# A planner without the rule that keeps VectorE's conversions and GpSimdE's operations apart

## The chip, the cores and the metric

The kernel runs on one core of one Trainium2 chip, in one launch. TensorE (PE) multiplies, VectorE (DVE), ScalarE (ACT) and GpSimdE (POOL) do the elementwise work, and SyncE (SP) issues the DMAs; each engine takes its instructions in the order in which they are written, and waits where an operand or a buffer is not ready. The metric is the device time of one execution in microseconds; less is better.

## The reference

Three parts in a row: a linear attention with the delta rule over 768 steps (4 batches, 8 heads, 48 elements), an expert layer with a rational function, and one with a squared relu. Each expert layer has 3072 tokens, 384 inputs and 2048 inner elements. Cut to what is computed:

```python
k_n = k / (np.linalg.norm(k, axis=-1, keepdims=True) + 1e-06)
for t in range(S):
    kt, vt, bt = (k_n[:, :, t], v[:, :, t], beta[:, :, t, None])
    y[:, :, t] = np.einsum('bhd,bhde->bhe', q[:, :, t], state)
    v_old = np.einsum('bhde,bhd->bhe', state, kt)
    state = state + bt[:, :, :, None] * np.einsum('bhd,bhe->bhde', kt, vt - v_old)
...
h = x @ w_in
P = a[0] + a[1] * h + a[2] * h2 + a[3] * h3
Q = 1.0 + np.abs(b[0]) * np.abs(h) + np.abs(b[1]) * h2
x = (P / (Q + 1e-06)) @ w_out
...
r = np.maximum(x @ w_in, 0.0)
return (r * r) @ w_out
```

Inputs and outputs are the host's arrays as they are; the expert weights arrive in 64-bit floating point and are turned into 32 bits on the chip with operations on integers.

## The kernel before

The 3072 tokens are cut into six stages of 512. For each stage i the attention of its steps is computed (group g = i, eight steps of 16 or 32 positions each), then layer 1 takes the stage's 512 columns through 16 pieces j of 128 inner elements. Layer 2 follows for all six stages.

The attention of a group has Gram products (L442, copied by ScalarE in L421), the norms (ScalarE L457, L458; VectorE L463 to L473, the head of the inverse), and the inverse of a triangular matrix. The inverse of g=0 and g=1 is a chain of 15 pairs of steps on VectorE (L479, L481), closed by two transposes (L514, L515); that of g=2 to 5 is a chain of 31 pairs on GpSimdE (L488, L492). Behind it TensorE takes the products L549, L560, L571, L597, L609 with copies by ScalarE (L429) or VectorE (L433) between, and VectorE's L553. Then come eight steps of the recurrence (TensorE L686, L745, L746; ScalarE L720, L739, L759; GpSimdE L724; VectorE L729, L764). GpSimdE scales the values in L641 and clears the tiles Tt and TT in L459 and L523.

One piece of layer 1 is: mm1 (L887, nine matmuls into one of three banks h), the rational function (ScalarE L904, L905, L906, then L910, L911 behind GpSimdE's L907; VectorE L908, L909, L912, L913 and L914, which writes the result), and mm2 (L923, three matmuls into the accumulators). Before a stage its columns are split into a high and a low part (ScalarE L870, VectorE L871). In layer 2 the function is L934 to L938 and the second product L947 to L949.

The weights of a piece come by DMA and are converted: ScalarE L829, VectorE L830, L831, L834 (the first matrix, A) and L836 (the second, B), then ScalarE L845 rounds A and GpSimdE L846 gives its low part.

No instruction is emitted directly. Every one is handed to a plan with its engine, an estimated duration, what it reads and writes, and a due time; conversions, steps of the inverse and several others carry `lock=1`. The plan's `play()` simulates the engines and always starts what can start earliest, with due times to choose; eight rounds are simulated, each with due times derived from the one before, and the order of the best is written out. Where the plan sees TensorE idle for long, filler matmuls (L283) are put there. No wait in the program enforces the plan's times; they only decide the order on each engine, which buffer an operation gets, and how many fillers there are.

## Time and profile before

| what | value |
|---|---|
| median of three runs | 1132.02 us (1125.41, 1132.02, 1133.59) |
| profiled execution | 1127.35 us |
| its span | 1125.6 us |
| TensorE busy | 1065.3 us, 95% |
| VectorE, ScalarE, GpSimdE busy | 673.7, 684.3, 387.8 us |
| mean granted TensorE clock | 0.966 |

All rows of the trace come from the one profiled execution. Times in it start with its span. A row of the timeline has the start, the length, the engine, the line, the operation, and the tiles with their shapes; "x3" joins three such instructions that follow each other, and the bracket at the end tells how long the engine was idle before and what it was released by. L907 in a row means line 907 of the kernel before.

### The profile page before, as it was taken

Reading aid. Unit: us, or ns where it says so; the run is one execution under the profiler, and the core shown is the slowest. Engines: PE = TensorE matmul, PEld = TensorE weight load, DVE = VectorE, ACT = ScalarE, POOL = GpSimd, SP = SyncE. Lnnn points to the kernel's source line nnn. Section 1 sums busy time; section 2 is a strip of 40 time slices with the busy share of each in tenths; the row PEclk is TensorE's granted clock in tenths of the full one; section 3 lists DMA queues with packets and bytes.
Section 4 is the critical chain, followed back from the end, with each engine's and each line's share of the span. In section 5 each row is a group of like instructions: output and inputs, shape, how many; then the busy total and the mean of one; then the engine's idle time right before and its main releaser. Section 6 shows DMA issues by size and latency. Waiting matters only on the chain.

```text
span 1125.6 us, 24712 instructions
## 1 busy us (share of the span) xinstructions
PE 1065.3 (95%) x10076; PEld 761.6 (68%) x10076; DVE 673.7 (60%) x1115; ACT 684.3 (61%) x1242; POOL 387.8 (34%) x540
## 2 busy tenths in 40 slices
PE   5688798789999999999999989999999999999998
PEld 5676565465666566666666556588888888888887
DVE  6567786777667756766666588887334343433332
ACT  4165687787788788777878697765334233332422
POOL 3314587628845862884233143425000000000000
PEclk7679899989999999999999999999999999999999
DMA  7464225560263055016000221441101010000000
GB/s 231 120 182 124 70 55 178 156 137 33 82 161 74 25 150 104 33 45 138 29 19 20 71 83 47 153 156 40 45 1 57 1 37 20 1 29 1 29 0 29
DMA packets 116065, 83.49 MB, mean 74 GB/s; under 512 B 83568, under 2 KB 101104, under 8 KB 115952
## 3 DMA queue, kind: packets, MB, share of 16 engines
q1 hardware_dynamic: 115952, 81.92, 25.5%
q8 instruction: 79, 1.29, 0.5%
q14 instruction: 34, 0.28, 0.1%
HBM read 62.88 MB, written 17.83 MB: 72 GB/s over the span
## 4 chain that ended last, share of the span: by engine, by line
PE 84%; ACT 4%; DVE 3%; issue 2%; POOL 0%; DMA 0%; SPq 0%; DVEq 0%; ACTq 0%; POOLq 0%
PE bank L887 34%; PE bank L923 21%; PE bank L949 6%; PE bank L947 6%; PE bank L948 6%; PE bank L686 5%; PE bank L745 2%; PE bank L597 1%; PE bank L609 1%; ACT mem L905 1%; ACT xin L759 1%; ACT mem L906 0%; DVE X L764 0%; ACT X L720 0%; DVE bank L913 0%
## 5 line engine op out<-in xcount | busy, mean ns | idle before, releaser
L887 PE MATMUL bank<-xh,A 128*128 128x512 f32 x1152 | 360.6, 394 | 1.1 <-POOL A L846 1.1
L923 PE MATMUL bank<-mem,B 128*128 128x512 f32 x576 | 278.6, 613 | 4.1 <-DVE mem L914 1.7
L887 PE MATMUL bank<-xl,A 128*128 128x512 f32 x576 | 257.6, 447 | 5.3 <-DVE mem L914 5.3
L887 PEld LDWEIGHTS bank<-xh,A 128*128 128x128 f32 x1152 | 218.4, 190 | 63.4 <-issue 16.0
L907 POOL TENSOR_TENSOR mem<-mem 128x512 f32<-128x512 f32 x96 | 123.3, 1286 | 203.6 <-ACT mem L905 203.0
L923 PEld LDWEIGHTS bank<-mem,B 128*128 128x128 f32 x576 | 103.8, 192 | 96.9 <-issue 78.7
L935 DVE SCALAR_TENSOR_TENSOR mem<-bank,mem 128x512 f32<-128x512 f32 x96 | 66.2, 690 | 157.0 <-ACT mem L934 157.0
L934 ACT ACTIVATE mem<-bank 128x512 f32<-128x512 f32 x96 | 57.3, 598 | 159.9 <-PE bank L887 158.0
L887 PEld LDWEIGHTS bank<-xl,A 128*128 128x128 f32 x576 | 109.1, 189 | 47.2 <-issue 15.3
L949 PE MATMUL bank<-gh,C 128*128 128x512 f32 x288 | 113.7, 395 | 0.0
L947 PE MATMUL bank<-gl,C 128*128 128x512 f32 x288 | 113.5, 394 | 0.0
L948 PE MATMUL bank<-gh,C 128*128 128x512 f32 x288 | 111.9, 389 | 0.0
L912 DVE SCALAR_TENSOR_TENSOR mem<-mem,par,bank 128x512 f32<-128x512 f32 x96 | 71.4, 743 | 67.0 <-ACT bank L911 66.8
L938 DVE TENSOR_TENSOR gl<-mem,gh 128x512 fp32r<-128x512 f32 x96 | 67.4, 702 | 61.3 <-ACT gh L937 61.2
L937 ACT CAST gh<-mem 128x512 fp32r<-128x512 f32 x96 | 59.6, 621 | 68.5 <-DVE mem L935 57.3
L908 DVE TENSOR_TENSOR mem<-bank,mem 128x512 f32<-128x512 f32 x96 | 65.8, 686 | 57.5 <-ACT mem L906 57.2
L904 ACT ACTIVATE mem<-bank 128x512 f32<-128x512 f32 x96 | 57.0, 595 | 47.5 <-PE bank L887 46.6
L905 ACT ACTIVATE mem<-mem,par 128x512 f32<-128x512 f32 x96 | 77.8, 812 | 2.0
L910 ACT ACTIVATE mem<-mem,par 128x512 f32<-128x512 f32 x96 | 69.3, 722 | 15.2 <-POOL mem L907 13.9
L906 ACT ACTIVATE mem<-bank,par 128x512 f32<-128x512 f32 x96 | 73.6, 769 | 0.7
L492 POOL TENSOR_TENSOR Tt<-Tt,tmp 128x31 f32<-128x31 f32 (+15 forms) x124 | 70.3, 567 | 8.5
L488 POOL TENSOR_TENSOR tmp<-Gb,Tt 128x31 f32<-128x31 f32 (+15 forms) x124 | 66.1, 533 | 20.1 <-DVE Tt L473 12.1
(125 smaller groups left out, 1564.7 us busy)
## 6 DMA issues: line engine op xcount, KB each, us to landing
raw<-in_w_dram SPq DMA_DIRECT2D x18, 768.0 KB, 4.6
B<-in_w_dram SPq DMA_DIRECT2D x10, 768.0 KB, 6.6
kTg<-in_kS_dram SPq DMA_DIRECT2D x40, 128.0 KB, 2.8
gs<-Gs SPq DMA_DIRECT2D x40, 128.0 KB, 2.8
kTc<-in_kT_dram SPq DMA_DIRECT2D x40, 128.0 KB, 2.4
X<-in_qT_dram SPq DMA_DIRECT2D x96, 48.0 KB, 2.6
kn<-in_kn_dram SPq DMA_DIRECT2D x12, 384.0 KB, 4.2
vn<-in_vn_dram SPq DMA_DIRECT2D x12, 384.0 KB, 3.5
```

Of the source, the lines that this page charges most:

```text
L492: P_.tensor_tensor(Tt[:, 0:a, s + 1:32], Tt[:, 0:a, s + 1:32], tv, op=ALU.subtract)
L887: M.matmul(h, a, b, start=(k == 0 and m == 0), stop=(k == NK - 1 and m == 2))
L905: add("ACT", 0.83, lambda: A_.activation(b(), a(), AF.Identity, bias=s(4), scale=s(5)), r=[ak, "par"], w=[bk], due=due + 3.3, alloc=(("b", ...
L906: add("ACT", 0.79, lambda: A_.activation(c(), h(), AF.Identity, bias=s(2), scale=s(3)), r=[hk, "par"], w=[ck], due=due + 4.5, alloc=(("c", ...
L907: add("POOL", 1.32, lambda: P_.tensor_tensor(b(), b(), a(), op=ALU.mult), r=[ak], w=[bk], due=due + 4.2, lock=1)
L910: add("ACT", 0.72, lambda: A_.activation(a(), b(), AF.Ln, bias=s(6)), r=[bk, "par6"], w=[ak], due=due + 6)
L912: add("DVE", 0.75, lambda: V.scalar_tensor_tensor(c(), c(), s(0), h(), op0=ALU.add, op1=ALU.mult), r=[hk, "par"], w=[ck], due=due + 8)
L923: M.matmul(acc[d], Bw[j][:, 128 * d:128 * d + 128], slot[gk], start=(j == 0), stop=(j == NJ - 1))
L938: add("DVE", 0.72, lambda: V.tensor_tensor(gl(), b(), gh(), op=ALU.subtract), r=[bk, gk, "late"], w=[lk], due=due + 5, lock=1, alloc=(("gl ...
L947: M.matmul(acc[d], wh, gl, start=(j == 0), stop=False)
L948: M.matmul(acc[d], wl, gh, start=False, stop=False)
L949: M.matmul(acc[d], wh, gh, start=False, stop=(j == NJ - 1))
```

## The change

The plan no longer keeps VectorE's operations marked `lock=1` and GpSimdE's from overlapping: the variable that held the end of the last such operation on either engine is gone. The planned durations of three conversions on VectorE are raised. The operations handed to the plan stay the same.

```diff
         kept, frees, owner, reuse = {}, {}, {}, {}
-        lockend = {"DVE": 0.0, "POOL": 0.0}
         for t in T:
...
                 s = max(s, a[len(t["alloc"]) - 1])
-            if t["lock"]:
-                s = max(s, lockend["POOL" if t["eng"] == "DVE" else "DVE"])
             return s
...
                 free_at[e] = end if e != "LAND" else 0.0
-            if t["lock"] and e in lockend:
-                lockend[e] = end
             t["s"], t["e"] = s, end
...
-            add("DVE", 0.56, lambda: V.tensor_scalar(lo(), lo(), 29, None, op0=ALU.logical_shift_right), w=[rk], due=d0, lock=1)
+            add("DVE", 0.62, lambda: V.tensor_scalar(lo(), lo(), 29, None, op0=ALU.logical_shift_right), w=[rk], due=d0, lock=1)
...
-            add("DVE", 0.6, lambda: V.scalar_tensor_tensor(lo()[:, si], hi()[:, si], 3, lo()[:, si], op0=ALU.logical_shift_left, op1=ALU.bitwise_or),
+            add("DVE", 0.7, lambda: V.scalar_tensor_tensor(lo()[:, si], hi()[:, si], 3, lo()[:, si], op0=ALU.logical_shift_left, op1=ALU.bitwise_or),
...
-            add("DVE", 0.6, lambda: V.scalar_tensor_tensor(Bw[j].bitcast(U32), hi()[:, so], 3, lo()[:, so], op0=ALU.logical_shift_left, op1=ALU.bitwise_or),
+            add("DVE", 0.7, lambda: V.scalar_tensor_tensor(Bw[j].bitcast(U32), hi()[:, so], 3, lo()[:, so], op0=ALU.logical_shift_left, op1=ALU.bitwise_or),
```

The orders of all four compute engines change in the first 240 us; the number of fillers falls from 124 to 89. The lines of the new kernel's body are lower by 5: its L899 is L904 of the kernel before, its L903 is L908.

VectorE at the beginning of the first stage of layer 1 (a bank is the h of one piece j; `mem` is the rational function's storage, `raw` and `B` the weights being converted), before:

```order
L908 TENSOR_TENSOR mem<-bank_74,mem 128x512
L909 SCALAR_TENSOR_TENSOR mem<-mem,par,bank_74 128x512
L908 TENSOR_TENSOR mem<-bank_72,mem 128x512
L909 SCALAR_TENSOR_TENSOR mem<-mem,par,bank_72 128x512
L908 TENSOR_TENSOR mem<-bank_73,mem 128x512
L912 SCALAR_TENSOR_TENSOR mem<-mem,par,bank_74 128x512
L463 RECIPROCAL nbr<-nby 128x32
L464 TENSOR_TENSOR nbr<-nbr,Gb 128x32
L465 TENSOR_TENSOR nbr<-nbr,nby 128x32
L466 TENSOR_SCALAR nrm<-nbr 128x32
L467 RECIPROCAL nbr<-nrm 128x32
L468 TENSOR_TENSOR nbr<-nbr 128x32
```

and in the changed kernel:

```order
L903 TENSOR_TENSOR mem<-bank_73,mem 128x512
L904 SCALAR_TENSOR_TENSOR mem<-mem,par,bank_73 128x512
L829 SCALAR_TENSOR_TENSOR raw_104<-raw_104 128x384
L907 SCALAR_TENSOR_TENSOR mem<-mem,par,bank_73 128x512
L908 SCALAR_TENSOR_TENSOR bank_73<-mem,bank_73 128x512
L825 TENSOR_SCALAR B<-B 128x768
L903 TENSOR_TENSOR mem<-bank_72,mem 128x512
L904 SCALAR_TENSOR_TENSOR mem<-mem,par,bank_72 128x512
L826 SCALAR_TENSOR_TENSOR B<-B 128x768
L831 SCALAR_TENSOR_TENSOR B<-mem 128x384
L909 SCALAR_TENSOR_TENSOR mem<-bank_73,mem 128x512
```

Before, L908 and L909 of two pieces, and L908 of a third, stand ahead of the first L912, and the head of the inverse of g=2 (L463 to L473) ahead of the first L913. Now the first piece goes through to its L914 (here L909), with conversions between, and the head of the inverse has moved behind the fifth piece's.

ScalarE at the same place (`Gs` is a Gram product's copy, TT_112 an operand of the attention of g=1), before:

```order
L905 ACTIVATE mem<-mem,par 128x512
L421 COPY Gs_139<-bank_75 128x256
L905 ACTIVATE mem<-mem,par 128x512 x2
L910 ACTIVATE mem<-mem,par 128x512 x2
L845 CAST A_83<-raw_103 128x384
L429 COPY TT_112<-bank_75 32x16x32
L910 ACTIVATE mem<-mem,par 128x512
L429 COPY TT_112<-bank_75 32x16x32 x3
L906 ACTIVATE mem<-bank_74,par 128x512
L906 ACTIVATE mem<-bank_72,par 128x512
L906 ACTIVATE mem<-bank_73,par 128x512
```

and in the changed kernel:

```order
L899 ACTIVATE mem<-bank_73 128x512
L900 ACTIVATE mem<-mem,par 128x512
L901 ACTIVATE mem<-bank_73,par 128x512
L899 ACTIVATE mem<-bank_72 128x512
L416 COPY Gs_138<-bank_75 128x256
L905 ACTIVATE mem<-mem,par 128x512
L906 ACTIVATE bank_73<-mem 128x512
L900 ACTIVATE mem<-mem,par 128x512
L416 COPY Gs_139<-bank_75 128x256
L901 ACTIVATE mem<-bank_72,par 128x512
```

Before, L905 and L910 of three pieces and the copies L429 stand ahead of the first L906; now the first piece has its five operations (here L899, L900, L901, L905, L906) almost in a row.

GpSimdE during the inverse of g=0 (X are the recurrence's operands, vn the values, A the first weights), before:

```order
L523 MEMSET TT_111 32x32x32 x2
L459 MEMSET Tt 128x1024
L641 TENSOR_TENSOR vn_130<-vn_130,nT_125 128x768
L724 AFFINE_SELECT X_107<-X_107 64x4x64 x2
L724 AFFINE_SELECT X_108<-X_108 64x4x64 x2
L724 AFFINE_SELECT X_109<-X_109 64x4x64 x2
L641 TENSOR_TENSOR vn_131<-vn_131,nT_125 128x768
L724 AFFINE_SELECT X_110<-X_110 64x4x64 x2
L846 TENSOR_TENSOR A_79<-mem,A_79 128x384
```

and in the changed kernel:

```order
L719 AFFINE_SELECT X_107<-X_107 64x4x64 x2
L518 MEMSET TT_111 32x32x32 x2
L719 AFFINE_SELECT X_108<-X_108 64x4x64 x2
L719 AFFINE_SELECT X_109<-X_109 64x4x64 x2
L719 AFFINE_SELECT X_110<-X_110 64x4x64 x2
L841 TENSOR_TENSOR A_79<-mem,A_79 128x384
L636 TENSOR_TENSOR vn_130<-vn_130,nT_125 128x768
L636 TENSOR_TENSOR vn_131<-vn_131,nT_125 128x768
L454 MEMSET Tt 128x1024
```

The memset of Tt (L459, here L454) stands behind the inverse on VectorE, whose result lies in Tt; before, the L641, L724 and L846 stood behind it, now (L636, L719, L841) ahead of it.

## Rows read from the trace of the kernel before

**Rows 1.** The page, part 1: busy time, share of the span and instructions of each engine.

```profile
PE 1065.3 (95%) x10076; PEld 761.6 (68%) x10076; DVE 673.7 (60%) x1115; ACT 684.3 (61%) x1242; POOL 387.8 (34%) x540
```

**Rows 2.** The table of windows, cut at the first mm1 of the stages of layer 1 (the second row is a part of the first). Columns: the window and its length; busy time and instructions of PE, PEld, DVE, ACT and POOL; granted TensorE clock; share of the DMA engines; GB/s.

```profile
96.00:240.50 144.50, 124.69 (x1828) 82.90 (x1827) 104.00 (x171) 102.57 (x191) 88.92 (x114) 0.92 0.43 121
131.00:240.50 109.50, 97.80 (x1162) 61.04 (x1162) 79.21 (x128) 80.83 (x152) 70.72 (x89) 0.94 0.48 137
341.40:441.80 100.40, 100.40 (x1137) 62.86 (x1137) 67.91 (x118) 82.06 (x153) 62.42 (x97) 1.00 0.37 88
643.70:735.00 91.30, 86.04 (x284) 53.88 (x283) 74.85 (x108) 72.18 (x115) 35.93 (x30) 0.98 0.33 114
```

**Rows 3.** TensorE from 96 to 131, grouped by line (busy time, mean ns of one, idle time before it and its releaser); then rows of its timeline (start, length, line; in brackets the idle time before the row).

```profile
L283 PE MATMUL bank<-ones 128*128 128x256 bf16 x61 | 7.5, 273 | 0.0
...
L571 PE MATMUL bank<-DN,mem 32*32 32x32 f32 x128 | 3.1, 214 | 2.1 <-ACT TT L429 2.1
...
L597 PE MATMUL bank<-TT,TN 32*32 32x32 f32 x64 | 1.2, 192 | 0.8 <-ACT TN L429 0.8
L609 PE MATMUL bank<-ws,TN 32*32 32x32 f32 x64 | 1.2, 192 | 0.4 <-ACT ws L429 0.4
...
95.95 0.50 PE L887 MATMUL bank<-xl,A 128*128 128x512 f32 x1
...
127.06 1.93 PE L560 MATMUL bank<-mem,DN 32*32 32x32 f32 x128 [4.43 <-DVE mem L553]
...
130.62 4.71 PE L923 MATMUL bank<-mem,B 128*128 128x512 f32 x6
```

**Rows 4.** ScalarE's timeline in the first stage.

```profile
103.67 1.09 ACT L904 ACTIVATE mem<-bank 128x512 f32<-128x512 f32 x2
...
107.70 1.52 ACT L905 ACTIVATE mem<-mem,par 128x512 f32<-128x512 f32 x2
109.12 1.57 ACT L910 ACTIVATE mem<-mem,par 128x512 f32<-128x512 f32 x2
...
114.25 2.12 ACT L906 ACTIVATE mem<-bank,par 128x512 f32<-128x512 f32 x3
...
116.77 0.58 ACT L911 ACTIVATE bank<-mem 128x512 f32<-128x512 f32 x1
```

**Rows 5.** VectorE's timeline in the first stage.

```profile
115.13 0.69 DVE L908 TENSOR_TENSOR mem<-bank,mem 128x512 f32<-128x512 f32 x1 [9.70 <-ACT mem L906]
...
119.16 0.34 DVE L463 RECIPROCAL nbr<-nby 128x32 f32<-128x32 f32 x1
...
122.37 0.69 DVE L913 SCALAR_TENSOR_TENSOR bank<-mem,bank 128x512 f32<-128x512 f32 x1
...
129.48 1.87 DVE L914 SCALAR_TENSOR_TENSOR mem<-bank,mem 128x512 f32<-128x512 f32 x3
```

**Rows 6.** GpSimdE in the first stage (96 to 240.5), grouped by line; then the two groups of the inverse in the second stage (240.5 to 341.4); then the first and the last of the 62 operations of the inverse of g=2 in its timeline.

```profile
L907 POOL TENSOR_TENSOR mem<-mem 128x512 f32<-128x512 f32 x16 | 20.5, 1288 | 19.4 <-ACT mem L905 19.2
L492 POOL TENSOR_TENSOR Tt<-Tt,tmp 128x31 f32<-128x31 f32 (+15 forms) x31 | 20.0, 647 | 2.1
L488 POOL TENSOR_TENSOR tmp<-Gb,Tt 128x31 f32<-128x31 f32 (+15 forms) x31 | 19.3, 624 | 5.4 <-DVE Tt L473 3.6
L846 POOL TENSOR_TENSOR A<-raw,A 128x384 fp32r<-128x384 f32 x10 | 10.4, 1036 | 15.9 <-ACT A L845 8.8 <-issue 7.0
L724 POOL TENSOR_SCALAR_AFFINE_SELECT X<-X 64x256 f32<-64x256 f32 x17 | 8.5, 500 | 4.4 <-ACT X L720 3.4 <-POOL X L724 0.5
...
L492 POOL TENSOR_TENSOR Tt<-Tt,tmp 128x31 f32<-128x31 f32 (+15 forms) x31 | 16.8, 541 | 2.2
L488 POOL TENSOR_TENSOR tmp<-Gb,Tt 128x31 f32<-128x31 f32 (+15 forms) x31 | 15.6, 503 | 3.4 <-DVE Tt L473 1.3
...
122.55 0.24 POOL L488 TENSOR_TENSOR tmp<-Gb,Tt 128x31 f32<-128x31 f32 x1 [3.64 <-DVE Tt L473]
...
212.24 0.99 POOL L492 TENSOR_TENSOR Tt<-Tt,tmp 128x31 f32<-128x31 f32 x1
```

**Rows 7.** The start: GpSimdE's timeline, then the ends of VectorE's inverse of g=0.

```profile
34.40 1.16 POOL L459 MEMSET Tt<- 128x1024 f32 x1 [14.96 <-DVE DN L515]
...
37.07 4.32 POOL L724 TENSOR_SCALAR_AFFINE_SELECT X<-X 64x256 f32<-64x256 f32 x6
...
20.36 1.23 DVE L472 TENSOR_TENSOR Gb<-Gb,nbr 128x1024 f32<-128x1024 f32 x1
...
32.36 1.93 DVE L515 STREAM_TRANSPOSE DN<-Tt 128x1024 f32<-128x1024 f32 x1
```

**Rows 8.** Operations of VectorE beside and not beside one of GpSimdE: L834 at 88.46 with GpSimdE's L641, and L834 at 99.61; L481 with 128x120 elements at 72.72 with GpSimdE's L724, and at 24.74.

```profile
88.46 1.35 DVE L834 SCALAR_TENSOR_TENSOR mem<-mem 128x384 uint32<-128x384 uint32 x1
...
99.61 0.55 DVE L834 SCALAR_TENSOR_TENSOR mem<-mem 128x384 uint32<-128x384 uint32 x1
...
87.92 1.47 POOL L641 TENSOR_TENSOR vn<-vn,nT 128x768 f32<-128x768 f32 x1 [3.77 <-issue]
...
72.72 0.45 DVE L481 TENSOR_TENSOR Tt<-Tt,tmp 128x120 f32<-128x120 f32 x1
...
72.63 0.41 POOL L724 TENSOR_SCALAR_AFFINE_SELECT X<-X 64x256 f32<-64x256 f32 x1 [27.75 <-PE bank L686]
...
24.74 0.28 DVE L481 TENSOR_TENSOR Tt<-Tt,tmp 128x120 f32<-128x120 f32 x1
```

## Prediction

> **What bounds the kernel now.** I read the page first: TensorE is busy for 1065.3 of 1125.6 us [rows 1]. Where is it not? The table of windows cut at the first mm1 of each stage of layer 1 (240.5, 341.4, ...) tells it [rows 2]: from 341.4 to 441.8 busy equals the window, and the last stage of layer 1 is busy for 86.04 of 91.3. Only the first stage is long: 144.5 us (96 to 240.5, 124.69 of them busy) against 100.4 for a later stage. Order can win time in the first 240 us, hardly after them.
>
> Next, what the first stage waits for. TensorE's list and timeline of 96 to 137 [rows 3]: the first mm1 starts at 95.95, and the first mm2 only at 130.62, behind the attention products L560 (127.06) that wait 4.43 us for VectorE. Between them stand 61 filler matmuls (7.5 us), which the plan puts where it sees a gap. ScalarE's rows [rows 4] tell why: L904 of three j's, then L905 of three, L910 of three, then copies for the attention (L429), and only at 114.25 the L906 without which VectorE cannot go on. VectorE [rows 5] sat idle for 9.70 us before L908 at 115.13, then took L463 to L473 (119.16 to 122.4, the head of the inverse of g=2) ahead of L913, and gave the first L914 at 129.48, 33 us after the mm1 it belongs to. So the stage is late by its order, not by a lack of engines.
>
> **The change, part by part.** No operation is added or removed except about 35 fillers (124 to 89); only the planned order differs, since nothing but order kept the two engines apart. I set the two orders side by side and priced three places.
>
> *First stage.* In the new order ScalarE takes j=0 through L904, L905, L906, L910, L911, with one L904 and one copy L421 between, VectorE follows with L908, L909, L912, L913, L914 and six other operations between, and the head L463 stands behind the fifth L914. By hand, the first mm1 at 97: its bank is complete at about 100; L904 0.6, L905 0.76 (1.52 for two), GpSimdE's L907 1.25 (3.74 for three), L910 0.78 (1.57 for two), L911 0.58 and the two inserted operations (1 us) bring ScalarE to 105.4; L912 and L913 at 0.7 each, six others of 0.55 to 1.0 (3.5 together) and L914 at 0.62 bring the first L914 to 111 [rows 4, 5]. That is 18 us earlier than 129.5 (rows give every term but the 100).
> What is left for TensorE then: its window from 131 to 240.5 holds 97.8 us of work and 11.7 of idle [rows 2]; the attention products L571, L597, L609 (3.1 + 1.2 + 1.2 = 5.5 us), which ran before 131, come after 111 too [rows 3]. TensorE alone would be through at 111 + 98 + 5.5 = 214.5, with the old idle at 226. But the inverse of g=2, 62 operations on GpSimdE, can no longer begin at 122.55 [rows 6]: its head is now behind five L914, some 29 VectorE rows of 0.2 to 1.0 us after the first L914, about 17 to 18 us with waits beside, plus the head's own 3.2 to 3.5 [rows 5]; so it starts at about 138, 15.5 later. By the order 7 L907, 5 L846 and 16 L724 lie inside it. From their rows: 19.3 + 20.0 for the inverse, 7 x 1.29, 5 x 1.04, 16 x 0.50, together 61.5, with up to 5 of gaps 66.5 [rows 6]. It ends at 199.5 to 204.5, against 213.2. Before, 27.3 us lay between that end and the next stage; if 17 of these are work that must follow, this road ends the stage at 216.5 to 221.5; with all 27.3 at 227 to 232. I take 228, nearest to the old idle (226) and inside the second figure: 131 us for the stage, a gain of 12.5 against the old 240.5. Bounds: 222 (gain 18) and, where the inverse is slowed by another 6 and the full tail follows, 238 (gain 2).
>
> *Start.* In the old plan GpSimdE was idle for 14.96 us, until 34.40, while VectorE ran the g=0 inverse, from L472 (20.36) to L515 (32.36, through at 34.3); then came the memset, two L641 six L724 (4.32 together) and L846 [rows 7]. In the new order L724 x8, an L846 and both L641 stand ahead of the memset, so they run beside that inverse, which is on the path to the first mm1. What does an overlap cost? The trace has one clean case [rows 8]: L834 took 1.35 at 88.46 while L641 ran from 87.92 to 89.39, and 0.55 alone at 99.61; an inverse step (L481) took 0.45 beside an L724 of 0.41, against 0.28 alone. The VectorE operation is held until the GpSimdE one ends. The price lies between 0 (all collide with nothing that waits) and the full length of what overlaps, 1.04 for L846 [rows 6], 2 x 1.47 for L641, six L724 at 0.41, together 6.4. I take 4 for the large three, 1 for the small ones: 5, near the full end because the inverse is one unbroken chain of some 35 VectorE rows. Behind it wait L514, L515 and with them TensorE's L549, L560.
> The Trainium skill (SBUF — State Buffer, section Who interferes with whom) says that VectorE and GpSimdE share a port pair that is held for a whole instruction, that a VectorE operation with two SBUF inputs contends with a GpSimdE operation that reads SBUF, and that one with at most one SBUF input, outside the two-port modes, does not. The L834 row agrees; by the rule alone the start would lose all 6.4 where the sum has 5.
> More filler matmuls stand ahead of the first mm1 and two products L549 are placed before it: 28 fillers at 7.5 / 61 are 3.4 us [rows 3], but they fill a wait, so I count 1 (bounds 0 and 3.4).
>
> *The rest.* The raised costs (0.56 to 0.62, 0.6 to 0.7) are only plan numbers. In stage 1 copies L457 and the Gb loads stand earlier; I allow 0 to 1 of gain. Stages 2 to 5 and layer 2 keep long identical stretches, and TensorE is full there, which hides any exchange of VectorE rows: 0. Should the cover fail, the last stage's 5.3 us of idle is what such a stage costs.
>
> *Sum.* -12.5 + 5 + 1 - 0 = -6.5 on the profiled execution: 1127.35 to about 1121. That execution lies 4.7 under the median of the three runs (1132.02; they run from 1125.41 to 1133.59). I go half the way up and say 1123. A difference of 1% (11.3 us) is about what this kernel's measurement tells from no change.
>
> **Rivals.**
> 1. *Only TensorE limits the first stage and the start hides the overlap.* For: GpSimdE's operations wait for inputs from VectorE and ScalarE, and many could fall beside VectorE rows that read only one tile. Against: the steps of the inverse, most rows there, read two. Stage gain 18, start +1: -17, or 1110.
> 2. *Nothing comes of it.* The early L914 is given back, since the inverse of g=2 starts 15.5 later and the mm1s end up waiting for A pieces (L846) behind it on GpSimdE. For: GpSimdE has 66 us in a row there. Against: before, that inverse took 90.7 us with the same operations and had slack. Stage gain 5 to 6, start +6: 1127 to 1132.
> 3. *Slower: the overlap costs in full, at every place.* One mechanism: a VectorE operation with two inputs in SBUF waits out the GpSimdE operation beside it, and the other way round. At the start 6.4; in the g=1 inverse, also VectorE's, two L846 and two L641 come beside it, 2 x 1.04 + 2 x 1.47 = 5; in the first stage the g=2 inverse, whose operations already lost 39.3 - 32.4 = 7 us against the next stage [rows 6], loses 7 more, and a stage limited by GpSimdE ends 7 later. -12.5 + 7 + 11.4 + 1 = +7: 1134 by the profile, 1138 by the median, up to 1146. It decides once the start loses more than the stage gains: more than about 12 us of overlap on the path, or half of that with a stage gain of only 5. By the page cited above this full price is the expected one; the trace bears it out in a handful of operations, so it has its chance below, no more.
>
> **How the numbers follow.** My forecast, a few us faster: 0.40 (its own range 1115 to 1129). Rival 1: 0.20. Rival 2: 0.20. Rival 3: 0.20. Faster by over 1% (below 1120.7) takes rival 1 and a quarter of my case: 0.30. Slower by over 1% (above 1143.3) is the upper end of rival 3: 0.10 with its half. The rest, 0.60, is within 1%. The range leaves out the tail of rival 1 and of rival 3: 1109 to 1140.
>
> **What would show it.** Right: in the changed kernel's trace the first mm2 follows the first mm1 by about 14 us instead of 34.7; the first stage is 127 to 136 us long instead of 144.5; the first mm1 comes at 99 to 103; fewer fillers after it; layer 2 about as long as before. In the g=0 inverse some VectorE rows are lengthened to the end of a GpSimdE row. Wrong: a first stage under 127 or over 140; a start later by more than 8 or not at all; a later stage that is 3 us or more longer than its 100, which I priced at nothing.

## The result, and the profile after

| | before | after |
|---|---|---|
| median | 1127.23 us (20 runs, 1120.12 to 1133.59) | 1135.36 us (20 runs, 1130.75 to 1141.96) |
| profiled execution | 1127.35 us | 1130.75 us |
| mean granted TensorE clock of it | 0.966 | 0.970 |

The ratio is 1.0074 with the interval [1.0057, 1.0091]: about 8 us slower, where 6.5 us faster was forecast between the profiled executions. The profiled execution of before lies at its median; that of after is the fastest of its 20. So two sums are kept apart below: the two traces differ by 3.4 us, the medians by 8.1.

The page of the changed kernel, part 1 [rows 1], and its windows [rows 2]: the first stage, a later stage, the last stage of layer 1, and 20 us around the first products of layer 2. Columns as in [rows 2].

```profile
PE 1068.4 (95%) x10041; PEld 760.0 (67%) x10041; DVE 689.3 (61%) x1115; ACT 683.4 (61%) x1242; POOL 397.2 (35%) x540
...
100.11:237.54 137.43, 122.36 (x1831) 78.57 (x1829) 100.63 (x160) 102.75 (x191) 85.55 (x112) 0.93 0.49 135
237.54:338.30 100.76, 99.42 (x1120) 62.09 (x1119) 73.40 (x122) 81.81 (x153) 64.17 (x96) 1.00 0.35 87
640.40:726.30 85.90, 78.83 (x247) 46.82 (x245) 73.18 (x102) 68.85 (x111) 38.77 (x30) 0.98 0.30 103
720.00:740.00 20.00, 16.02 (x60) 10.69 (x59) 19.43 (x21) 12.74 (x23) 13.95 (x10) 1.00 0.83 291
```

The same 20 us of the kernel before:

```profile
720.00:740.00 20.00, 20.00 (x78) 14.23 (x77) 16.95 (x24) 13.45 (x25) 7.15 (x7) 1.00 0.77 277
```

The first mm1 of the second and of the fifth stage before, and of the fifth stage after:

```profile
239.96 0.79 PE L887 MATMUL bank<-xl,A 128*128 128x512 f32 x1
...
541.32 0.79 PE L887 MATMUL bank<-xl,A 128*128 128x512 f32 x1
...
539.51 0.79 PE L882 MATMUL bank<-xl,A 128*128 128x512 f32 x1
```

The same operations take VectorE 15.6 us longer (689.3 against 673.7) and GpSimdE 9.4 longer: the overlap lengthens them. Cut at the first mm1 of each stage, the two traces differ at four places: the first mm1 comes 4.16 us later (100.11 against 95.95 [rows 3]); the first stage is 6.6 us shorter (137.43 against 144.01, 95.95 to 239.96); the next three stages give back 0.6, so that the fifth stage begins 1.8 earlier than before; and on the way into layer 2 TensorE loses 5.2, after which layer 2 stays 3.4 late to the end. In the two windows of 720 to 740 is the surprise: TensorE, full before, now has 3.98 us of idle in 20, and VectorE is busy for 19.43 of them. The orders differ there too: they change not only in the first 240 us, but at places in the later stages, and on all engines again between 650 and 795.

**The start.** Timelines of the changed kernel [rows 7]: GpSimdE's rows beside the inverse of g=0, VectorE's steps beside them and one of the same shape later, and TensorE's first product behind the inverse.

```profile
18.67 3.66 POOL L719 TENSOR_SCALAR_AFFINE_SELECT X<-X 64x256 f32<-64x256 f32 x6
22.42 1.08 POOL L841 TENSOR_TENSOR A<-mem,A 128x384 fp32r<-128x384 f32 x1
23.46 2.97 POOL L636 TENSOR_TENSOR vn<-vn,nT 128x768 f32<-128x768 f32 x2
...
22.66 0.92 DVE L476 TENSOR_TENSOR Tt<-Tt,tmp 128x56 f32<-128x56 f32 x1
23.61 1.42 DVE L474 TENSOR_TENSOR tmp<-Gb,Tt 128x78 f32<-128x78 f32 x1
25.07 1.46 DVE L476 TENSOR_TENSOR Tt<-Tt,tmp 128x78 f32<-128x78 f32 x1
...
32.47 0.24 DVE L476 TENSOR_TENSOR Tt<-Tt,tmp 128x78 f32<-128x78 f32 x1
...
35.55 1.88 DVE L510 STREAM_TRANSPOSE DN<-Tt 128x1024 f32<-128x1024 f32 x1
...
35.80 1.92 PE L544 MATMUL bank<-Gb,mem 32*32 32x32 f32 x127 [5.51 <-DVE Gb L509]
```

Two steps of 0.24 us take 1.42 and 1.46, and each ends where a L636 ends; a third waits out L841. The 30 steps together take 11.23 us instead of 7.64. The inverse is through at 37.4 instead of 34.3, and TensorE stands idle for 5.51 us.

**The first stage.** The first piece, now early [rows 3, 5]; the head of the inverse of g=2 on VectorE; that inverse on GpSimdE, first and last row, and GpSimdE's groups of 100 to 237.5 [rows 6]:

```profile
100.11 0.48 PE L882 MATMUL bank<-xl,A 128*128 128x512 f32 x1
...
113.84 2.41 PE L918 MATMUL bank<-mem,B 128*128 128x512 f32 x5 [2.50 <-DVE mem L909]
...
139.62 0.35 DVE L458 RECIPROCAL nbr<-nby 128x32 f32<-128x32 f32 x1 [1.91 <-ACT nby L453]
141.55 2.01 DVE L467 TENSOR_TENSOR Gb<-Gb,nbr 128x1024 f32<-128x1024 f32 x1
143.48 1.00 DVE L468 COPY Tt<-nbr 128x32 f32<-128x32 f32 x1
...
144.62 0.24 POOL L483 TENSOR_TENSOR tmp<-Gb,Tt 128x31 f32<-128x31 f32 x1 [0.18 <-POOL A L841]
...
209.67 0.27 POOL L487 TENSOR_TENSOR Tt<-Tt,tmp 128x31 f32<-128x31 f32 x1
...
L483 POOL TENSOR_TENSOR tmp<-Gb,Tt 128x31 f32<-128x31 f32 (+15 forms) x31 | 19.2, 621 | 2.3 <-POOL A L841 0.2
L487 POOL TENSOR_TENSOR Tt<-Tt,tmp 128x31 f32<-128x31 f32 (+15 forms) x31 | 19.1, 617 | 1.8
```

The first mm2 follows the first mm1 by 13.7 us (14 was forecast, 34.7 stood before). The inverse starts at 144.62 (138 was forecast), lasts 65.3 us and ends at 209.9; 27.6 us later the next stage begins.

**The way into layer 2.** VectorE, GpSimdE and TensorE of the changed kernel from 720 on. L825, L826 convert layer 2's weights; L866 makes the low part xl that its first mm1s need.

```profile
720.29 1.61 DVE L826 SCALAR_TENSOR_TENSOR raw<-raw 128x768 uint32<-128x768 uint32 x1
721.82 1.37 DVE L825 TENSOR_SCALAR B<-B 128x768 uint32<-128x768 uint32 x1
723.30 1.60 DVE L826 SCALAR_TENSOR_TENSOR B<-B 128x768 uint32<-128x768 uint32 x1
724.82 1.50 DVE L866 TENSOR_TENSOR xl<-xin,xh 128x512 fp32r<-128x512 f32 x1
726.24 0.55 DVE L825 TENSOR_SCALAR B<-B 128x768 uint32<-128x768 uint32 x1
726.89 0.96 DVE L826 SCALAR_TENSOR_TENSOR B<-B 128x768 uint32<-128x768 uint32 x1
727.77 0.68 DVE L866 TENSOR_TENSOR xl<-xin,xh 128x512 fp32r<-128x512 f32 x1
...
720.05 1.03 POOL L841 TENSOR_TENSOR A<-B,A 128x384 fp32r<-128x384 f32 x1 [3.63 <-ACT A L840]
721.03 1.74 POOL L848 TENSOR_TENSOR C<-B,C 128x384 fp32r<-128x384 f32 x1
722.74 1.35 POOL L841 TENSOR_TENSOR A<-raw,A 128x384 fp32r<-128x384 f32 x1
724.04 1.72 POOL L848 TENSOR_TENSOR C<-raw,C 128x384 fp32r<-128x384 f32 x1
...
726.37 0.50 PE L882 MATMUL bank<-xl,A 128*128 128x512 f32 x1 [1.67 <-DVE xl L866]
728.51 0.50 PE L882 MATMUL bank<-xl,A 128*128 128x512 f32 x1 [1.17 <-DVE xl L866]
734.70 0.50 PE L942 MATMUL bank<-gl,C 128*128 128x512 f32 x1 [1.14 <-DVE gl L933]
```

Four GpSimdE operations in a row, four VectorE operations beside them, each 0.6 to 0.8 us longer than alone: 2.9 us together, while VectorE has no idle time to take them from. TensorE's three waits (1.67 + 1.17 + 1.14) are the 3.98 of the window. The kernel before is not free of it, since the rule holds in the plan and not on the chip: there one L846 and one L853 (721.05 to 723.9) stand beside two lengthened rows, 1.4 us together.

```profile
721.43 1.59 DVE L831 SCALAR_TENSOR_TENSOR raw<-raw 128x768 uint32<-128x768 uint32 x1
722.94 1.50 DVE L871 TENSOR_TENSOR xl<-xin,xh 128x512 fp32r<-128x512 f32 x1
```

Over 640 to 740, VectorE is busy for 79.76 us before and 86.42 after.
The Trainium skill (SBUF — State Buffer, section Who interferes with whom) says that a VectorE operation with two SBUF inputs, which L826 and L866 are, contends with a GpSimdE operation that reads SBUF, and that tensor_scalar can contend where it runs in a two-port mode. Their rows agree, and the 1.37 us of the one-input L825, 0.55 alone, fits the second; no run here shows in which mode it ran.

### The profile page after: what moved, and what is told of

It is laid out like the page before. It is cut to its first block, busy times and chain, and to the rows that moved or that the text cites. A ratio compares the mean times of both kernels' runs of the same rounds, so it can differ in the third digit from the quotient of the medians.

```text
span 1129.0 us, 24629 instructions
## 1 busy us (share of the span) xinstructions
PE 1068.4 (95%) x10041; PEld 760.0 (67%) x10041; DVE 689.3 (61%) x1115; ACT 683.4 (61%) x1242; POOL 397.2 (35%) x540
## 4 chain that ended last, share of the span: by engine, by line
PE 76%; POOL 5%; ACT 5%; DVE 4%; issue 3%; POOLq 0%; ACTq 0%; DVEq 0%
PE bank L882 31%; PE bank L918 17%; PE bank L944 6%; PE bank L942 6%; PE bank L943 6%; PE bank L681 5%; PE bank L740 2%; POOL mem L902 2%; POOL Tt L487 1%; POOL tmp L483 1%; ACT mem L900 1%; PE bank L592 1%; PE bank L604 1%; ACT mem L905 1%; ACT bank L906 1%
## 5 line engine op out<-in xcount | busy, mean ns | idle before, releaser
L902 POOL TENSOR_TENSOR mem<-mem 128x512 f32<-128x512 f32 x96 | 126.5, 1318 | 204.6 <-ACT mem L900 204.6
L907 DVE SCALAR_TENSOR_TENSOR mem<-mem,par,bank 128x512 f32<-128x512 f32 x96 | 71.5, 745 | 72.9 <-ACT bank L906 72.6
L933 DVE TENSOR_TENSOR gl<-mem,gh 128x512 fp32r<-128x512 f32 x96 | 70.6, 736 | 65.1 <-ACT gh L932 65.0
L905 ACT ACTIVATE mem<-mem,par 128x512 f32<-128x512 f32 x96 | 69.4, 723 | 36.6 <-POOL mem L902 35.6
L903 DVE TENSOR_TENSOR mem<-bank,mem 128x512 f32<-128x512 f32 x96 | 65.8, 685 | 36.5 <-ACT mem L901 36.0
L900 ACT ACTIVATE mem<-mem,par 128x512 f32<-128x512 f32 x96 | 77.8, 810 | 1.8
L899 ACT ACTIVATE mem<-bank 128x512 f32<-128x512 f32 x96 | 57.0, 593 | 28.9 <-PE bank L882 28.1
L901 ACT ACTIVATE mem<-bank,par 128x512 f32<-128x512 f32 x96 | 73.9, 769 | 0.9
L904 DVE SCALAR_TENSOR_TENSOR mem<-mem,par,bank 128x512 f32<-128x512 f32 x96 | 71.6, 746 | 2.7
```

Source lines behind the costliest of these rows:

```text
L900: add("ACT", 0.83, lambda: A_.activation(b(), a(), AF.Identity, bias=s(4), scale=s(5)), r=[ak, "par"], w=[bk], due=due + 3.3, alloc=(("b", ...
L901: add("ACT", 0.79, lambda: A_.activation(c(), h(), AF.Identity, bias=s(2), scale=s(3)), r=[hk, "par"], w=[ck], due=due + 4.5, alloc=(("c", ...
L902: add("POOL", 1.32, lambda: P_.tensor_tensor(b(), b(), a(), op=ALU.mult), r=[ak], w=[bk], due=due + 4.2, lock=1)
L904: add("DVE", 0.75, lambda: V.scalar_tensor_tensor(c(), c(), s(1), h(), op0=ALU.add, op1=ALU.mult), r=[hk, "par"], w=[ck], due=due + 6.3)
L905: add("ACT", 0.72, lambda: A_.activation(a(), b(), AF.Ln, bias=s(6)), r=[bk, "par6"], w=[ak], due=due + 6)
L907: add("DVE", 0.75, lambda: V.scalar_tensor_tensor(c(), c(), s(0), h(), op0=ALU.add, op1=ALU.mult), r=[hk, "par"], w=[ck], due=due + 8)
```

## The experiments

Ratios are to the kernel before on the same chip, with their 95% interval; the difference of two of them is uncertain by about 3 us. Lines in a short diff are those of the kernel it starts from, and "..." stands for lines left out.

**Is the overlap at the start on the path?** e11 takes it away from the changed kernel; e12 gives it, and hardly anything else, to the kernel before. In e11 the first L841 and two L636 are written behind the memset of Tt:

```diff
+        three, at = [self.a0[0]] + self.vs[:2], self.order.index(self.tt[1])
...
+        self.order = [i for i in self.order[:at + 1] if i not in three] + three + self.order[at + 1:]
```

> The changed kernel with three GpSimdE operations of the start (the low part of the first A, L841, and the two scalings of the values, L636) written behind the memset of Tt (L454) instead of ahead of it, so that they come after the inverse of g=0; nothing else moves. Theory A (in the changed kernel the steps of the inverse beside them took 0.92, 1.42 and 1.46 us instead of 0.22 to 0.24): these three rows fall back to 0.24, the first mm1 and the whole come about 3 us earlier, ratio to the kernel before 1.0045 to 1.005. Rival (the start waits for something else, the memset and A pieces being late then): no gain, 1.0074.

1.0031 [1.0014, 1.0049], 1129.64 us. Its timeline (lines of the kernel before): the second transpose and TensorE's first product behind the inverse.

```profile
33.22 1.91 DVE L515 STREAM_TRANSPOSE DN<-Tt 128x1024 f32<-128x1024 f32 x1
...
33.48 1.71 PE L549 MATMUL bank<-Gb,mem 32*32 32x32 f32 x127 [1.44 <-DVE Gb L514]
```

The inverse ends at 35.1 and the 5.51 us of idle shrink to 1.44. By the ratios the overlap costs (1.0074 - 1.0031) x 1127 = 4.8 us. In this one execution the first mm1 (99.76) is hardly earlier than that of after: its xl are begun 1.0 us earlier (95.4 against 96.4), but the 28 fillers ahead of it stand in between in both. The spans are equal too (1129.2 and 1129.0), so only the medians show the gain.

e12, in the kernel before, moves the memset of Tt behind the L641, L724 and L846:

```diff
+        at = self.order.index(self.tt[1])
+        to = self.order.index(self.a0[0])
...
+        self.order = self.order[:at] + self.order[at + 1:to + 1] + [self.tt[1]] + self.order[to + 1:]
```

> The kernel before with one instruction moved: the memset of Tt (L459) stands behind the seven GpSimdE rows that followed it, so that L641, L724 and L846 may run beside the inverse of g=0, as in the changed kernel. Theory A: steps of the inverse are lengthened by up to 2 x 1.47 for L641 and some more for L724, if their inputs are there by then; the first mm1 and the whole 3 to 4 us later, ratio 1.003. Rival: that inverse has slack in the kernel before and the ratio is 1.000.

1.0037 [1.0020, 1.0055], 1130.35 us: 4.2 us slower. Its rows (lines higher by 6 than before):

```profile
36.95 1.89 DVE L521 STREAM_TRANSPOSE DN<-Tt 128x1024 f32<-128x1024 f32 x1
...
37.20 1.92 PE L555 MATMUL bank<-Gb,mem 32*32 32x32 f32 x126 [5.83 <-DVE Gb L520]
```

The inverse ends at 38.8 instead of 34.3, the first mm1 comes at 99.11. This execution, the slowest of its 12, does not carry those 3.2 us on: its first stage is 2.4 us shorter than before's, and its second one 4.9 us longer (105.8). Given or taken, the overlap at the start is worth 4 to 5 us in the medians; where in the run they are lost, the traces do not show.

**Is the overlap before layer 2 on the path?** e3 keeps the rule from the plan's time 600 on; until then its order is that of the changed kernel.

```diff
+            if t["lock"] and s > 600:
+                s = max(s, lockend["POOL" if t["eng"] == "DVE" else "DVE"])
```

> The changed kernel, but the plan keeps VectorE's and GpSimdE's marked operations apart again from its time 600 on (the last stage of layer 1 and the passage to layer 2). On every engine the order up to there is that of the changed kernel, with the same 89 fillers. Theory A (the loss lies in the passage from layer 1 to layer 2, where the three L871 of layer 2 stand behind lengthened conversions and TensorE waits 1.67 + 1.17 + 1.14 us for them): the 4.9 us lost there come back, about 1130 where the changed kernel has 1135, and TensorE is idle for less than 1 us from 720 to 740. Rival B (the loss is TensorE's clock, lower with 35 fewer fillers): as the changed kernel, 1135, ratio 1.007. Rival C (both, about half each): 1130 to 1131, and still 3 us above the kernel before.

1.0041 [1.0021, 1.0061], 1131.25 us: 3.7 us of the 8 are back. Its window of 720 to 740:

```profile
720.00:740.00 20.00, 19.43 (x66) 12.13 (x65) 16.24 (x22) 13.79 (x25) 7.62 (x7) 1.00 0.81 274
```

TensorE is busy for 19.43 instead of 16.02, and from the first mm1 of the fifth stage to the end it loses 0.7 us instead of 5.2. All the kept traces agree with this: that stretch takes 584.2 to 586.3 us in the nine kernels whose plan keeps the rule from 600 on (before: 584.3), and 587.0 to 592.2 in the eleven that don't. One caution comes from this run: its order is the same as after's in the first 100 us, yet its first L904 (L899 of after) starts at 107.80 and not at 102.52. Single executions differ by 5 us there.

e15 has both (e3 and e11), with all other orders left.

> The changed kernel with two things undone: the marked operations are kept apart in the plan from its time 600 on, and the three GpSimdE operations of the start stand behind the memset; all fillers stay. Theory A (both overlaps are what the change loses, 3.7 and 4.8 us one by one): they add up, ratio 0.998 to 1.001. If the first stage of layer 1 gains on its own what its rows show (138 us instead of 144.5) and nothing else eats it: 0.994 to 0.997. If the two price the same wait twice: 1.003.

1.0020 [1.0004, 1.0035], 1126.55 us. The two overlaps are 6.1 of the 8.3 us, with all 89 fillers in place. That lies between theory A (0.998 to 1.001) and a wait priced twice (1.003); 0.994 to 0.997, by which the first stage's gain would show on its own, is excluded. e13 has in addition at most 4 fillers ahead of the first mm1, where after has 28:

```diff
+                n = min(n, 4) if 80 < T[i]["s"] < 90 else n
```

> The changed kernel with three things undone at once: the marked operations are kept apart in the plan from its time 600 on, the three GpSimdE operations of the start stand behind the memset, and 4 instead of 28 fillers stand ahead of the first mm1. The order of the first stage of layer 1 stays that of the changed kernel. If theories A and D hold and add up: 3.7 + 3 + 2.5 us under the changed kernel, ratio 0.998 to 1.000, or 2 us better than the kernel before at most. If the first stage gives back what is won ahead of it: 1.003.

1.0023 [1.0006, 1.0040]: no different from e15. e14 has that edit alone, in the changed kernel:

> The changed kernel with 4 fillers instead of 28 right ahead of the first mm1 (65 in all); nothing else moves. Theory D (these 28 matmuls, 4.7 us in the changed kernel's trace, stand in the way: the three xl were done at 98.3 and the first mm1 began at 100.1): the first mm1 2 to 3 us earlier, ratio 1.005. Rival B (fewer fillers mean a lower clock behind them): 1.008 to 1.010, with a granted clock of 0.5 in the first mm1s.

1.0108 [1.0074, 1.0142], 1138.44 us. The first mm1 came at 97.70, but the inverse of g=2 began at 144.34, as in after, and the stage ended at 235.95. The ratio is near rival B's, and the granted clock is 0.70 in 97.70 to 105, where after has 1.00 in 100.11 to 107. The fillers ahead of the first mm1 are not the cause of the loss.

**The number of fillers (89 for 124).** e4 makes the plan count a filler as 0.12 instead of 0.16 us in the changed kernel, which gives 122; e7 counts 0.22 in the kernel before, which gives 87.

```diff
-    PL.fill = (T0 - 64, T0 + 20, lambda: nc.tensor.matmul(banks[2][:, 0:N // 2], ones[:, 0:128], ones, start=True, stop=True), 0.16, FILL)
+    PL.fill = (T0 - 64, T0 + 20, lambda: nc.tensor.matmul(banks[2][:, 0:N // 2], ones[:, 0:128], ones, start=True, stop=True), 0.12, FILL)
```

> The changed kernel with the planned length of a filler set to 0.12 instead of 0.16, so that 122 fillers are put where it has 89 (the kernel before has 124). All other instructions stand in the same order. Theory A (passage to layer 2): no gain, 1135 or a few us more, ratio 1.007 or above. Rival B (35 fewer fillers, and so a lower clock, make the loss): mean granted clock back from 0.961 to about 0.966, and 1128 to 1131. Rival C: 1131 to 1132.

1.0083 [1.0051, 1.0114], 1134.99 us: nothing regained. But the mean clock of its runs stays at 0.962, so this run tests the number of fillers and not the clock.

> The kernel before with the planned length of a filler set to 0.22, so that 87 fillers are put instead of 124; all else in the same order. Theory A: fillers only fill waits, ratio 1.000. Rival B: slower by 4 to 8 us with a lower mean clock, ratio 1.004 to 1.007.

1.0065 [1.0041, 1.0088], 1132.82 us: the kernel before does lose 7 us by it, and its runs have a mean clock of 0.961 against 0.967. Its trace, of the fastest of its 12 runs, does not show where. So the number matters in the order of before, and more of them did not help the order of after, 38 of whose fillers then stand right ahead of the first mm1. Over other orders the number decides nothing (e1 below, 67 fillers: 0.9988); that it has a share in what e15 leaves is not excluded.

**Is the first stage limited by the inverse of g=2?** e5 keeps the rule until the plan's time 88 only (`s < 88`).

> The changed kernel, but the plan keeps the marked operations of the two engines apart up to its time 88, that is until the first mm1; it puts 129 fillers. If the overlap at the start costs what the trace shows (the inverse of g=0 lengthened by 3.9 us, the first mm1 at 100.1 instead of 95.95), the first mm1 comes at about 96 and the run is 4 us faster than the changed kernel, 1131, by theory A, which has the passage to layer 2 still costing 4.9. Rival B has the fillers as well: 1127 or below. If the start costs nothing in the end, because the first stage waits for GpSimdE's inverse anyway: 1135.

1.0053 [1.0033, 1.0072], 1131.97 us. The head of that inverse came early again; its last row, and the first mm1 of the second stage:

```profile
179.75 0.65 POOL L492 TENSOR_TENSOR Tt<-Tt,tmp 128x31 f32<-128x31 f32 x1
...
234.92 0.79 PE L887 MATMUL bank<-xl,A 128*128 128x512 f32 x1
```

The inverse ends 30 us earlier than after's, and the stage is as long (98.05 to 234.92, 136.9 us). So the inverse plus a fixed tail does not by itself set the end of this stage. On the start this run tells nothing: the plan kept the rule, but on the chip two L641 ran beside the inverse of g=0, with steps of 1.50 and 1.55 us, and it was through only at 36.8. e18 writes the head and its two norms on ScalarE ahead of the fifth L907 to L909 and two copies, in the changed kernel:

```diff
+        six = sorted(self.head[2], key=self.order.index)
...
+        self.order = self.order[:to] + six + [i for i in self.order[to:] if i not in six]
```

> The changed kernel with six instructions groups moved: the norms of g=2 (ScalarE L452, L453) stand ahead of the two copies L424 that hold them up, and VectorE's head of that inverse (L458 to L468) ahead of L907 to L909 of the fifth piece; nothing else moves. Theory E (the first stage ends some 27 us after the inverse of g=2, so that its start decides): the inverse starts 3 to 4 us earlier than 44.5 us after the first mm1, the stage is as much shorter than 137.4, ratio 1.004. Rival (TensorE or the conversions limit the stage): the stage stays at 137 or grows by the 3 us that the fifth L909 is late, ratio 1.0074 to 1.010.

1.0085 [1.0060, 1.0111]. The inverse still began 45.6 us after the first mm1, with its inputs late; the edit did not move what it was meant to move, and tells nothing.

**The rule or the durations?** The change has two parts. e2 raises the three planned durations and keeps the rule (the last three pairs of lines of the diff, alone).

> Only the second part of the change: the three raised durations in the plan (0.62, 0.7, 0.7), the two engines kept apart throughout as in the kernel before; 109 fillers. Theory A (the loss comes from overlaps): ratio 1.000 to 1.002. Rival (any new order of the start loses, by its fillers and waits): 1.004 or above.

1.0107 [1.0083, 1.0131], 1136.77 us: with no overlap allowed in the plan, 12 us slower. Its first stage by windows, with the 30 us at its beginning, and TensorE's groups in it that wait:

```profile
96.75:252.05 155.30, 133.47 (x1815) 88.12 (x1812) 112.12 (x180) 108.08 (x199) 87.23 (x115) 0.87 0.43 116
100.00:130.00 30.00, 22.98 (x675) 20.20 (x675) 20.10 (x38) 23.08 (x41) 16.49 (x25) 0.76 0.28 67
...
L745 PE MATMUL bank<-X 112*48 112x64 f32 x64 | 6.2, 236 | 4.8 <-ACT X L739 4.8
...
L571 PE MATMUL bank<-DN,mem 32*32 32x32 f32 x128 | 3.1, 214 | 6.2 <-ACT TT L429 6.2
```

The stage is 155.3 us long instead of 144.0. TensorE's idle time is only 2.0 us of these 11.3 (21.8 against 19.8), though it now falls on ScalarE's copies L429 and L739, which come late. The other 9.3 are busy time, 133.47 against 124.19 for about as many matmuls, at a granted clock of 0.87 against 0.92: it is at its lower level from 115.6 to 136.1, behind the first of two waits for L429.

e1 was to be the other half, the rule removed and the old durations. By an oversight it also has 0.6 instead of 0.7 for the planned durations of L913 and L914 of the rational function, so it is not the rule alone:

```diff
-        add("DVE", 0.7, lambda: V.scalar_tensor_tensor(h(), b(), 1.0 + EPS, h(), op0=ALU.add, op1=ALU.mult), r=[bk], w=[hk], due=due + 8.8, free=[bk])
+        add("DVE", 0.6, lambda: V.scalar_tensor_tensor(h(), b(), 1.0 + EPS, h(), op0=ALU.add, op1=ALU.mult), r=[bk], w=[hk], due=due + 8.8, free=[bk])
```

> Only the first part of the change: nothing kept apart, the old durations; 67 fillers. Theory A: both overlaps are there, so a loss like that of the changed kernel, ratio 1.006 to 1.010, with lengthened steps of the inverse of g=0 and lengthened conversions at the passage to layer 2. Rival (the raised durations make the loss): 1.000 to 1.002.

0.9988 [0.9971, 1.0005], 1123.80 us; first stage 129.3 us. e19 (the rule removed and 0.56 raised to 0.62) has the same oversight in it:

> Nothing kept apart, and of the three durations only that of L830 raised (0.62). Of the two theories on the raised durations: if raising them spoils the first stage by a rule (conversions look dearer, the head of the inverse goes later), the result lies between 0.9988 (none raised) and 1.0074 (all raised); if each new plan is a draw of its own, it may lie outside.

1.0042 [1.0019, 1.0064]. e20, free of it, has the rule removed and only the two raises to 0.7:

> Nothing kept apart, and of the three durations only those of L834 and L836 raised (0.7). As for the run with 0.62 alone: between 0.9988 and 1.0074 if there is a rule, anywhere from 0.990 to 1.012 if each plan is a draw of its own.

1.0027 [1.0011, 1.0042], 1129.38 us. Then the two runs without the oversight: e23, the rule removed and nothing else (the diff's first three pieces, alone), and e24, besides only the raise to 0.62.

> The kernel before with the rule removed from the plan and every planned duration left alone; the run called e1_nolock_oldcost had, by an oversight, also 0.6 instead of 0.7 for two operations of the rational function (L913, L914 of the kernel before), so it did not test the rule alone. 68 fillers; the head of the inverse of g=2 stands behind the fifth L909, as in the changed kernel. Theory A (the raised planned durations cost the 8 us, the rule's removal by itself costs nothing): 1122 to 1128, ratio 0.996 to 1.001, first stage 129 to 134 us, the conversions before layer 2 not lengthened by more than 2 us together. Theory B (the removal of the rule costs by itself, by the overlap at the start and before layer 2; the good time of e1_nolock_oldcost came from the two lowered durations): 1130 to 1137, ratio 1.003 to 1.009, first stage 135 to 139, and rows of 1.4 to 1.6 us among the conversions at 715 to 727.

1.0031 [1.0013, 1.0049], 1130.48 us. First stage 134.5 us (101.40 to 235.88), and from the fifth stage into layer 2 a loss of 4.0 us. What e1 had seemed to show, that the rule's removal costs nothing, falls with this run.

> The changed kernel with only the raise from 0.56 to 0.62 kept (the run called e19_nolock_062 had the two lowered durations of the rational function as well). 62 fillers. Theory A: between the rule removed alone and the changed kernel, ratio 1.002 to 1.006, first stage 133 to 137. Theory B (order by chance: any small change of a planned duration moves the time by some us in either direction): anything from 0.997 to 1.009, and no relation to the sum of the single raises.

1.0061 [1.0041, 1.0081], 1133.11 us, with a first stage of 129.8 us and a loss of 7.1 us into layer 2. Together:

| planned durations | rule kept | rule removed |
|---|---|---|
| as before | 1 | 1.0031 (e23) |
| 0.62 only | not run | 1.0061 (e24) |
| 0.7 only | not run | 1.0027 (e20) |
| all raised | 1.0107 (e2) | 1.0074 (the change) |
| as before, two others lowered | not run | 0.9988 (e1) |
| 0.62 only, two others lowered | not run | 1.0042 (e19) |

Removing the rule costs 3.5 us with the old durations and gains 3.7 with the new; raising them costs 12 us with the rule and 4.8 without; lowering two other numbers by 0.1 gains 4.8 (e1 against e23) or 2.1 (e19 against e24). These effects do not add up.

**Better orders.** e9 keeps the rule except between 40 and 600 of the plan's time (`not 40 < s < 600`), with the raised durations; e17 does so with the old ones.

> The plan itself keeps the marked operations apart where overlap costs, up to its time 40 and from 600 on, and not between; the raised durations; 103 fillers. Theory A: neither overlap is there, ratio 0.996 to 1.001, with the first stage of layer 1 shorter than 144.5 us. If the new order of the first stage is what loses: 1.003 or above.

0.9984 [0.9966, 1.0002], 1122.52 us; first stage 133.6 us, a loss of 0.7 us into layer 2.

> The kernel before with the old durations, the marked operations kept apart in the plan up to its time 40 and from 600 on, and not between. Theory A2 (the two overlaps cost 3 to 5 us each wherever they fall on a chain that is waited for, and the raised durations spoil the order of the first stage): like the kernel with nothing kept apart and old durations (0.9988), less the overlap at its start, so 0.992 to 0.997. Rival (the order of each new plan scatters by 10 us either way, whatever its rule): anywhere from 0.990 to 1.010.

0.9981 [0.9961, 1.0001], 1123.24 us. With the rule where the overlap was seen to hurt and without it in between, the kernel is about 2 us faster than before at best; both intervals include no change. In e17, though, the rule held at the start in the plan only. A step of the inverse beside a L641 (20.76 to 22.2):

```profile
20.78 1.50 DVE L481 TENSOR_TENSOR Tt<-Tt,tmp 128x30 f32<-128x30 f32 x1
```

Its inverse of g=0 is through at 37.0, nearly as late as after's, where e9's is at 34.5; yet its first mm1 comes at 95.83, and the two medians are alike. So the 4 to 5 us of the start are no fixed price that every order pays.

## Why the prediction was wrong

**"The rest: 0" failed.** The step was that TensorE is full in the later stages and layer 2, "which hides any exchange of VectorE rows". TensorE was full there, but fed just in time: at the way into layer 2 VectorE was already busy for 16.95 of 20 us, and the overlap took the rest. The cost is 5.2 us between the traces and, by e3, 3.7 in the medians. Of the prediction's signs it was "layer 2 about as long as before" that failed: from its first mm1 (724.91 before, 723.43 after) to the end it takes 405.6 us instead of 400.7. The later stages of layer 1, for which it had set a bound of 3 us, lose 0.6 together from the second to the fourth.

**The first stage was mis-sized: 6.6 us instead of 12.5.** (In lengths the prediction has 13.5, 144.5 to 131: the 12.5 is the end of the stage, with the first mm1 taken at 97 for 96, and this 1 us was counted again in the start.) Its first half was right (first mm2 13.7 us after the first mm1; the inverse of g=2 lasting 65.3 us, in the 61.5 to 66.5 given). Measured from the first mm1, 6.4 us are missing: the inverse began 3.5 later than taken, behind ScalarE's norm L453 and a L467 and L468 lengthened beside a L841 (2.01 and 1.00 us), and was 1.2 shorter than the upper figure; and the tail was 27.6 where 23.5 had been taken, nearly the full one that [rows 6] show. But e5, with the inverse through 30 us earlier and a stage as long, shows that this road was not the only one to the end of the stage. What sets the end in each order is open.

**The start was right in size: 4.2 to 4.8 us for 5 + 1.** The inverse is lengthened as [rows 8] have it, by 3.6 us. How this reaches the first mm1 is less clear: it comes at 100.11 in after, at 99.76 without the overlap (e11), at 97.70 without 24 of the fillers (e14) and at 97.07 without either (e13), in single executions that differ by as much. In the medians taking the overlap away gains, and taking the fillers away gains nothing (e13, e14).

**"The raised costs are only plan numbers" was true of the chip and false of the plan.** They change no operation, but they choose the order: alone they lose 12 us (e2). The prediction read the resulting order at three places and priced the rest at nothing, without asking which part of the change made which order.

**The sum.** Between the traces: +4.2 - 6.6 + 0.6 + 5.2 = +3.4, which is the difference of the spans (1129.0 - 1125.6). The other 4.7 us to the medians' 8.1 are the good luck of the profiled execution of after. Over its 20 runs, time goes with the mean clock (correlation -0.78; 0.961 on average, 0.970 in the profiled one); in the runs of before on each chip it does so less (-0.22 to -0.44). Some of the difference between executions lies in the first 100 us, as e3 shows, and some elsewhere: e14, with after's order behind the first mm1, has a second stage of 105.3 us instead of 101.6. For the runs without a trace only a time and a mean clock are on record.

**The rivals.** Rival 3 had the sign and, with 1134 to 1146, the time; the forecast's own 1115 to 1129 did not, so that the whole range holds 1135 only through this rival. Its mechanism, a VectorE operation waiting out the GpSimdE operation beside it, is in the rows above, and e3, e11, e12 and e15 show that it costs. Its places were only partly right: the start cost 4 to 5 and not 6.4, the inverse of g=1 took 7.85 us for 7.74 and lost none of its 5, that of g=2 did not lose 7 more, and the dearest place it did not name. Rival 2's stage gain of 5 to 6 and start of +6 came near, but it too had nothing before layer 2. Rival 1 is refuted by the 4.16 us at the first mm1 and a stage gain of 6.6 for its 18.

**What stays open.** e15 leaves 2.2 us (ratio 1.0020) that neither overlap explains, and the 6.6 us that after's trace gains in the first stage are missing besides. The mean clock goes along with the times (0.967 before on the chip of e3, 0.961 after, 0.962 in e3, 0.966 in e11); whether it is more than a consequence of the waits, no run separates. And e23 and after differ by 4.8 us in the medians, while in their traces layer 2 runs equally late (3.3 and 3.4 us), so that no place can be named for what the raised durations add to the rule's removal.

## What to carry to other kernels

A full engine hides other engines' work only as long as its feeder has slack: ahead of every passage (a layer's first products) read how busy the feeder is in a window of 10 to 20 us, and if it is near what it was here (17 of 20), price an overlap on it in full. A rule that holds in a plan need not hold on the chip: look in the trace for what it was to keep apart. In a planned order a duration is not an estimate that may be corrected at will but a number that picks the order; time each part of such a change alone, since here 0.06 to 0.1 us on paper moved the kernel by up to 12 us. And before a few us between two traces are explained, see where both executions lie among their own runs.

## What was not expected of the hardware

A VectorE step of 0.24 us took 1.42 and 1.46 us beside GpSimdE's L636 of 1.48 (six times as much), while the L826 of 0.96 took 1.60 beside operations of 1.03 to 1.74: in these rows the time lost does not grow with the VectorE operation's own length, so short steps lose the most for their size. An operation with a single input, L825, was lengthened as well, from 0.55 to 1.37 us.

The granted TensorE clock from 40 to 95 us differed between the traces of these orders: 0.73 before, 0.69 after, 0.66 in e2, as means over its two levels (1.2 and 2.4 GHz). These are single executions; e3 and e18, whose order up to there is after's, have 0.69 too. The windows, in this order:

```profile
40.00:95.00 55.00, 41.61 (x1397) 37.10 (x1397) 33.19 (x82) 28.62 (x67) 13.18 (x20) 0.73 0.63 172
...
40.00:95.00 55.00, 42.61 (x1527) 38.27 (x1527) 37.57 (x84) 26.38 (x62) 11.42 (x15) 0.69 0.58 158
...
40.00:95.00 55.00, 42.03 (x1317) 37.14 (x1318) 31.64 (x80) 27.80 (x65) 11.49 (x16) 0.66 0.62 171
```

In e2 it was also low within the first stage, 0.76 in 100 to 130 against 0.90 before. TensorE waited there twice for ScalarE's copies L429, for 2.06 us (until 113.03) and for 4.18 us (until 124.83); the clock fell at 115.6, between the two, and rose at 136.1.
